# Attention with mixed heads, then two MLPs, on one core: the scores of the third and fourth chunk made at other steps, q and other loads issued at other places

## The chip, the cores and the metric

One core of a Trainium2 chip runs the whole program. The metric is the device time of one execution in microseconds (us); lower is better. Five engines work side by side, each in its own program order: TensorE (PE, with its weight loads PEld), VectorE (DVE), ScalarE (ACT), GpSimd (POOL), and SyncE (SP), which here only issues DMAs.

## The reference

Batch 2, 12 heads, 448 tokens, head size 64. Cut to what the change touches:

```python
scores = scale * np.matmul(q, k.transpose(0, 1, 3, 2))
scores = np.einsum('bhij,hg->bgij', scores, w_pre)
scores = scores - np.max(scores, axis=-1, keepdims=True)
attn = np.exp(scores)
attn = attn / (np.sum(attn, axis=-1, keepdims=True) + 1e-09)
attn = np.einsum('bhij,hg->bgij', attn, w_post)
return np.matmul(attn, v)
```

The result, as 2 x 448 tokens of 768 channels, goes through a token-and-channel-mixing MLP and then a gated MLP with a spatial gate. Neither is touched by the change.

## The kernel before, in words

**Chunks.** The query tokens of each batch are cut into four chunks (120, 120, 120 and 88 tokens), eight chunks in all, numbered x = 0 to 7. `qk(x, i)` makes the scores of head pair i (0 to 5) of chunk x: eight PE matmul instructions into a PSUM tile of two banks, and a copy of 128x896 numbers to the chunk's tile `S`, by ACT or, where the call names it, by DVE. There are two PSUM pools, psM and psB, of two such tiles each; `post` and `av` take theirs from psM, `pre` from psB.

**Steps.** A chunk is worked off in steps of 20 tokens: 6, 6, 6 and 5 per batch, 46 steps in all; chunk 2 begins at step 12, chunk 3 at step 18, chunk 4 at step 23. Each step has these parts: `b_dma` (two DMAs on SP gather the step's rows out of `S` into two of the eight ring tiles `P`, 210 KB each), `b_pre` (eight matmuls mix the heads with w_pre), `b_max` (DVE), `b_exp` (two ACT exponentials with their sums), `b_norm` (POOL: reciprocal of the sums, and w_post scaled by it), `b_post` (56 small matmuls that mix the heads with w_post and transpose), and `b_turn` (DVE copies the result into `AT`).

**Order.** The program is written out by hand in one loop over i from -5 to 45, and every engine runs its part in that order. Round i holds, in this order: `pre` of step i+2; the first `qk` that is due; `max` of i+2; `norm` of i+1; the other `qk` that are due; `post` of step i; `exp` of i+2; `turn` of i; an `av` (attention times v, 80 PE instructions) if one is due; the gather `b_dma` of step i+5; the loads listed for round i; and one move of the weight conversion (`pump`). So a gather is issued some four steps ahead of the `pre` that reads it, and `exp` of a step must be done before `pre` of two steps later may overwrite its PSUM tile.

**Scores and loads before.** Chunks 0 and 1 are scored ahead of the loop. Chunk 2's six `qk` come at rounds 1 to 6, chunk 3's at 7 to 12, chunk 4's at 13 to 17 with two at 13, and those of chunks 5 to 7 one per round at 18 to 35. Loads of q (192 KB), k (224 KB), v (512 KB) and the first weight piece (512 KB) stand in the table `loads` by round. The next batch's k tile i takes the place of this batch's, so it waits for `qk(3, i)`.

Tile names in the traces: `qk<-kn,qn` are the score matmuls, `S<-qk` their copies, `pre<-P,wp`, `nm<-pre` (max), `E<-pre,nm` (exp), `rc`, `rr`, `wt` (norm), `post<-wt,E`, `AT<-post` (turn), `av<-AT,vn`.

Of the kernel before, what the change touches and what calls it, by code (L numbers as in the profile page):

```python
# [20 lines left out]
LD, LP = 5, 2  # L21
# [10 lines left out]
def tile_kernel(ctx, tc, q, k, v, w_pre, w_post, w_tok1, w_tok2, w_ch1, w_ch2,  # L32
# [4 lines left out]
    NP = H // 2  # L37
# [136 lines left out]
    def pump(n):  # L174

        for _ in range(n):
            if wstate["conv"] < wstate["room"]:
                next(wstate["steps"], None)
# [110 lines left out]
    psM = actx.enter_context(tc.tile_pool(name="psM", bufs=2, space=PSUM))  # L289
# [11 lines left out]
    NQ = NP // QG  # L301
# [5 lines left out]
    def load_q(b, c, g, eng=nc.sync):  # L307
        t = qn[b, c, g] = qp.tile([P, QG, P], F32, tag=f"qn{g}", name=f"qn{b}_{c}_{g}", bufs=2)
        eng.dma_start(out=t, in_=q[b, :, c, g * QG:(g + 1) * QG])
# [28 lines left out]
    first = {}  # L338
# [6 lines left out]
    NB = len(steps)  # L345
# [173 lines left out]
    def add(step, fn, *a):  # L519
        extra.setdefault(step, []).append((fn, a))  # L520

    chunks = [(b, c) for b in range(B) for c in range(len(CH))]
# [25 lines left out]
    turn_over(8)  # L548

    COPIES = (nc.vector.tensor_copy,), (nc.scalar.copy,)  # L550
    scores = {}
    for x in range(NCH):
        if x < 2:
            at = [-LD - 1 + x] * NP
            for i in range(NP):
                n = x * NP + i
                add(at[i], qk, x, i, (psM, psB)[n % 2], COPIES[n % 2])
        else:
            f0, f1 = first[chunks[x - 1]] - LD, first[chunks[x]] - LD
            room = list(range(f0, f1))  # L560
            at = [room[i * len(room) // NP] for i in range(NP)]
            for i in range(NP):
                scores.setdefault(at[i], []).append((x, i))
        if x == 0:
            add(at[-1], scale_pre)
    for fn, a in extra.pop(-LD - 1):
        fn(*a)
    loads = {}
    for at, fn, *a in [(-4, load_q, 0, 2, 0), (-3, load_q, 0, 2, 1), (2, load_v, 0, 0), (4, load_q, 0, 3, 0),
                       (6, load_q, 0, 3, 1), (8, load_k, 1, 0), (9, load_q, 1, 0, 0), (9, load_k, 1, 1),  # L570
                       (10, load_k, 1, 2), (11, load_k, 1, 3), (12, load_v, 0, 1), (12, load_k, 1, 4), (13, load_k, 1, 5),
                       (10, load_q, 1, 0, 1), (14, load_v, 0, 2), (10, w_dma),
                       (15, load_const_late), (15, load_q, 1, 1, 0), (16, load_q, 1, 1, 1),
                       (18, load_q, 1, 2, 0), (20, load_q, 1, 2, 1), (24, load_v, 1, 0), (23, load_q, 1, 3, 0),
                       (26, load_v, 1, 1), (25, load_q, 1, 3, 1), (28, load_v, 1, 2)]:
        loads.setdefault(at, []).append((fn, a))
# [5 lines left out]
    TURNS_AT = {(-4, 1), (-3, 1), (-2, 1), (0, 1), (1, 1), (3, 1), (4, 1)}  # L582

    END = NB - LD
    PUMPS = {i: 1 + (i in ()) for i in range(14, NB)}
    LAST = ((0, 1, 2), (3, 4, 5))
    LAST_AT = (0, 1)
    MID_AT = (0, 3, 5)
# [1 line left out]
    for x in range(0, NCH - 2, 2):  # L590
        f0, f1 = first[chunks[x + 2]], first[chunks[x + 3]]
# [13 lines left out]
    for i in range(-LD, NB):  # L605
# [29 lines left out]
        if wstate["conv"] <= p_t2[-1]:  # L635
            pump(PUMPS.get(i, 0))
        if i + LD == first[chunks[-1]] - 1:
# [389 lines left out]
def build(shapes, manual=True):  # L1027
    import concourse.bacc as _bacc
    import concourse.tile as _tile
    import numpy as _np  # L1030
    from concourse import mybir as _mybir

    nc = _bacc.Bacc("TRN2", target_bir_lowering=False, num_devices=1, dynamic_dma_scratch_size=1024)
    args = []
    for name, (shape, dtype) in shapes.items():
        args.append(nc.dram_tensor(f"in_{name}_dram", shape, _mybir.dt.from_np(dtype), kind="ExternalInput").ap())
    for i, (shape, dtype) in enumerate(_OUTS):
        dt = _mybir.dt.from_np(_np.dtype(dtype))
        args.append(nc.dram_tensor(f"out_{i}_dram", shape, dt, kind="ExternalOutput").ap())
    with _tile.TileContext(nc) as tc:  # L1040
        if manual:
            with tc.manual_schedule():
                tile_kernel(tc, *args)
        else:
            tile_kernel(tc, *args)
    return nc
# [12 lines left out]
```

## Time and profile before

| what | value |
|---|---|
| three runs, us | 495.44, 498.73, 502.58 (median 498.73) |
| the profiled execution | 498.87 us |
| its span, first to last instruction | 497.1 us |
| granted TensorE clock, mean | 1.000 |
| PE busy | 477.4 us, 96% |
| DVE, ACT, POOL busy | 69%, 47%, 43% |
| mean DMA rate | 129 GB/s |

Attention takes roughly the first 183 us and the two MLPs the rest. "issue" in a profile row is time in which an engine waited for nothing that the profile shows. The busy time of PE is modelled and matmuls overlap, so 96% does not say that PE could not do the same work in less time.

### The profile page before, as it was taken

How to read it: one execution, taken by the hardware profiler on the slowest of the kernel's cores; microseconds unless marked ns; L12 is line 12 of the kernel's file. 1: busy time of each engine (PE TensorE's matmuls, PEld its weight loads, DVE VectorE, ACT ScalarE, POOL GpSimd, SP SyncE). 2: the span in 40 equal slices, each digit the busy share in tenths (PEclk: the TensorE clock that was granted, in tenths of full speed). 3: DMA queues.
4: the chain of work that ended last, by engine and by line, in shares of the span. 5: the costliest groups of instructions: out<-in, count | busy, mean ns of one | idle time of the engine just before them, and what ended most of it. 6: DMA issues, size and time to landing. Idle time of an engine off the chain costs nothing.

```text
span 497.1 us, 12963 instructions
## 1 busy us (share of the span) xinstructions
PE 477.4 (96%) x5482; PEld 390.2 (78%) x5482; DVE 340.7 (69%) x454; ACT 232.1 (47%) x452; POOL 211.4 (43%) x305
## 2 busy tenths in 40 slices
PE   9998899998899979999999999999999999999997
PEld 5455555555566879999999999999999998888996
DVE  3666547755775638836576678788788865897882
ACT  3577556856765435634344443333332444455320
POOL 2354544745555311581233242454445633258500
PEclk9999999999999999999999999999999999999999
DMA  5677953765443302302244253434532414004222
GB/s 181 229 235 236 264 179 119 244 204 203 162 168 100 159 4 65 127 1 69 101 127 135 98 185 113 128 106 128 172 103 86 124 57 140 20 0 128 79 79 108
DMA packets 26302, 64.17 MB, mean 129 GB/s; under 512 B 2900, under 2 KB 19844, under 8 KB 26244
## 3 DMA queue, kind: packets, MB, share of 16 engines
q1 hardware_dynamic: 26100, 63.14, 38.9%
q8 instruction: 43, 0.70, 0.6%
q10 hardware_dynamic: 144, 0.20, 0.1%
q14 instruction: 15, 0.12, 0.1%
HBM read 41.22 MB, written 2.75 MB: 88 GB/s over the span
## 4 chain that ended last, share of the span: by engine, by line
PE 87%; DVE 4%; ACT 4%; issue 3%; DMA 1%; POOL 0%; SPq 0%; POOLq 0%; ACTq 0%; DVEq 0%
PE qk L329 7%; PE av L483 6%; PE pre L369 6%; PE c2ps L662 6%; PE c1ps L662 6%; PE c2ps L664 6%; PE c1ps L664 6%; PE c1ps L663 6%; PE c2ps L663 6%; PE post L416 5%; PE av L465 2%; PE ups L663 2%; PE ups L662 2%; PE ups L664 2%; PE vps L663 2%
## 5 line engine op out<-in xcount | busy, mean ns | idle before, releaser
L157 POOL TENSOR_TENSOR wl<-cv,wh 128x768 fp32r<-128x768 f32 x28 | 53.2, 1899 | 125.1 <-ACT wh L154 93.5
L416 PEld LDWEIGHTS post<-wt,E 60*64 60x64 f32 x2520 | 46.5, 134 | 31.6 <-issue 20.1
L382 ACT ACTIVATE E<-pre,nm 128x448 f32<-128x448 f32 x90 | 56.5, 636 | 18.0 <-DVE nm L374 16.4
L416 PE MATMUL post<-wt,E 60*64 60x60 f32 x2520 | 49.9, 219 | 9.0 <-issue 7.5
L434 DVE COPY AT<-post 128x840 f32<-128x840 f32 x43 | 44.2, 1031 | 19.7 <-PE post L416 19.7
L374 DVE TENSOR_REDUCE nm<-pre 128x2 f32<-128x896 f32 (+1 forms) x46 | 48.9, 1063 | 6.9 <-PE pre L369 6.4
L369 PE MATMUL pre<-P,wp 64*64 64x448 f32 (+1 forms) x360 | 51.0, 543 | 1.7 <-DMA P<-S 0.6
L334 ACT COPY S<-qk 128x896 f32<-128x896 f32 x42 | 38.0, 907 | 31.1 <-PE qk L329 31.1
L136 DVE SCALAR_TENSOR_TENSOR cv<-raw,cv 128x768 uint32<-128x768 uint32 (+2 forms) x44 | 51.5, 1170 | 1.2
L662 PE MATMUL c1ps<-uh,wh 128*128 128x448 f32 x144 | 52.3, 363 | 0.0
L662 PE MATMUL c2ps<-r1h,wh 128*128 128x448 f32 x144 | 52.3, 363 | 0.0
L664 PE MATMUL c1ps<-uh,wl 128*128 128x448 f32 x144 | 52.2, 362 | 0.0
L664 PE MATMUL c2ps<-r1h,wl 128*128 128x448 f32 x144 | 52.2, 362 | 0.0
L663 PE MATMUL c1ps<-ul,wh 128*128 128x448 f32 x144 | 51.8, 360 | 0.0
L663 PE MATMUL c2ps<-r1l,wh 128*128 128x448 f32 x144 | 51.8, 360 | 0.0
L114 ACT ACTIVATE cv<-raw 128x768 f32<-128x768 f32 (+2 forms) x44 | 36.1, 822 | 27.8 <-POOL wl L157 20.7
L329 PE MATMUL qk<-kn,qn 64*64 64x448 f32 x384 | 48.1, 548 | 0.0
L138 DVE SCALAR_TENSOR_TENSOR cv<-raw,cv 128x768 uint32<-128x768 uint32 (+2 forms) x44 | 41.9, 951 | 1.0
L389 POOL TENSOR_SCALAR rc<-sm 128x2 f32<-128x2 f32 (+1 forms) x46 | 10.6, 231 | 73.5 <-ACT E L382 73.2
L154 ACT CAST wh<-cv 128x768 fp32r<-128x768 f32 x28 | 23.4, 836 | 34.8 <-DVE cv L138 33.8
L685 DVE SCALAR_TENSOR_TENSOR r1l<-c1ps,r1h 128x448 fp32r<-128x448 f32 x24 | 15.0, 624 | 30.6 <-ACT r1h L683 30.6
L391 POOL TENSOR_TENSOR rr<-rc,mone 128x2 f32<-128x2 f32 (+1 forms) x46 | 32.4, 705 | 3.8
(151 smaller groups left out, 1015.1 us busy)
## 6 DMA issues: line engine op xcount, KB each, us to landing
P<-S SPq DMA_DIRECT2D x88, 210.0 KB
raw<-in_w_ch_dram SPq DMA_DIRECT2D x24, 768.0 KB
vn<-in_v_dram SPq DMA_DIRECT2D x6, 512.0 KB
raw<-in_w_v_dram SPq DMA_DIRECT2D x6, 512.0 KB
raw<-in_w_u_dram SPq DMA_DIRECT2D x4, 768.0 KB
raw<-in_w_out_dram SPq DMA_DIRECT2D x6, 512.0 KB
qn<-in_q_dram SPq DMA_DIRECT2D x15, 192.0 KB
kn<-in_k_dram SPq DMA_DIRECT2D x12, 224.0 KB
```

What stands on the lines that cost most here:

```text
L136: nc.vector.scalar_tensor_tensor(fi, lo, 29, fi, op0=ALU.logical_shift_right, op1=ALU.bitwise_or)
L138: nc.vector.scalar_tensor_tensor(fi, hi, 0xC0000000, fi, op0=ALU.bitwise_and, op1=ALU.bitwise_or)
L157: nc.gpsimd.tensor_tensor(dst[1], f, f32(dst[0]), op=ALU.subtract)
L329: nc.tensor.matmul(ps[cols, j, :S], lhsT=qn[b, c, i // QG][rows, i % QG, cols], rhs=KX[b, i][rows], start=True, stop=True)
L369: nc.tensor.matmul(ps[cols, e, :S], lhsT=wp[rs], rhs=ring[(2 * i + r) % NP_BUFS][rs], start=True, stop=True)
L374: nc.vector.tensor_reduce(out=st[i]["nm"][:, :ne], in_=st[i]["pre"][:, :ne, :S], axis=AX.X, op=ALU.max, negate=True)
L382: nc.scalar.activation(t, st[i]["pre"][:, e, :S], AF.Exp, bias=st[i]["nm"][:, e:e + 1], scale=1.0, accum_out=sm[:, e:e + 1])
L416: nc.tensor.matmul(ps[HALVES[x], r, o:o + HW], lhsT=st[i]["e"][e][rs, t * 64:(t + 1) * 64], rhs=st[i]["w"][e][rs, :HW], start=True, stop=True)
L434: copy(dst, src)
L662: nc.tensor.matmul(ps, lhsT=lh, rhs=rh, start=(start and i == 0), stop=False)
L663: nc.tensor.matmul(ps, lhsT=lh, rhs=rl, start=False, stop=False)
L664: nc.tensor.matmul(ps, lhsT=ll, rhs=rh, start=False, stop=(stop and i == n - 1))
```

## The change

Three tables of the loop are written anew.

1. `QK_AT` says at which round each `qk` of chunks 2 to 7 is made. Chunk 2: rounds -2, -2, -1, -1, 0 and 1; those at rounds up to 0 are copied by ACT and DVE in turn, where all were copied by ACT. Chunk 3: rounds 3, 5, 7, 9, 11, 12. Chunk 4: as before. Chunk 5: two at 18, then 19 to 22. Chunks 6 and 7: each one round earlier, 23 to 28 and 29 to 34.
2. Chunk 2's q is loaded right behind the scores of chunk 0, ahead of the first gather; chunk 3's q at rounds 1 and 5 instead of 4 and 6; the first v tile at 9 instead of 2; the k tiles of the second batch at 10 to 15 instead of 8 to 13; its first q at 11 and 13 instead of 9 and 10; the first weight piece at 13 instead of 10.
3. The weight conversion begins at round 16 instead of 14 and makes two moves at rounds 20 and 30, so that the number of moves is the same.

```diff
     COPIES = (nc.vector.tensor_copy,), (nc.scalar.copy,)
+    QK_AT = [[-2, -2, -1, -1, 0, 1], [3, 5, 7, 9, 11, 12], [13, 13, 14, 15, 16, 17], [18, 18, 19, 20, 21, 22], [23, 24, 25, 26, 27, 28], [29, 30, 31, 32, 33, 34]]
     scores = {}
...
         else:
-            f0, f1 = first[chunks[x - 1]] - LD, first[chunks[x]] - LD
-            room = list(range(f0, f1))
-            at = [room[i * len(room) // NP] for i in range(NP)]
+            at = QK_AT[x - 2]
             for i in range(NP):
-                scores.setdefault(at[i], []).append((x, i))
+                scores.setdefault(at[i], []).append((x, i, psM, COPIES[1 - i % 2]) if at[i] <= 0 else (x, i))
...
+    for g in range(NQ):
+        load_q(0, 2, g)
     loads = {}
-    for at, fn, *a in [(-4, load_q, 0, 2, 0), (-3, load_q, 0, 2, 1), (2, load_v, 0, 0), (4, load_q, 0, 3, 0),
-                       (6, load_q, 0, 3, 1), (8, load_k, 1, 0), (9, load_q, 1, 0, 0), (9, load_k, 1, 1),
...
+    for at, fn, *a in [(1, load_q, 0, 3, 0), (5, load_q, 0, 3, 1),(9, load_v, 0, 0), (10, load_k, 1, 0), (11, load_q, 1, 0, 0), (11, load_k, 1, 1),
+                       (12, load_k, 1, 2), (12, load_v, 0, 1), (13, load_k, 1, 3), (13, load_q, 1, 0, 1),
...
-    PUMPS = {i: 1 + (i in ()) for i in range(14, NB)}
+    PUMPS = {i: 1 + (i in (20, 30)) for i in range(16, NB)}
```

PE ahead of the first `post`, before the change (`pre0` is `pre` of step 0; `qk0_2_3` is batch 0, chunk 2, head pair 3):

```order
 L329 MATMUL qk0_1_5_213<-kn0_5_117,qn0_1_1_121 64x448 x4
 L369 MATMUL pre0_229<-P0_93,wp_69 64x448 x2
 L369 MATMUL pre0_229<-P1_94,wp_69 64x448 x2
 L369 MATMUL pre1_243<-P2_95,wp_69 64x448 x2
 L369 MATMUL pre1_243<-P3_96,wp_69 64x448 x2
 L369 MATMUL pre2_265<-P4_97,wp_69 64x448 x2
 L369 MATMUL pre2_265<-P5_98,wp_69 64x448 x2
 L416 MATMUL post0_280<-wt0_0_254,E0_0_237 64x60 x12
```

The same place after it:

```order
 L329 MATMUL qk0_1_5_217<-kn0_5_117,qn0_1_1_121 64x448 x4
 L369 MATMUL pre0_229<-P0_93,wp_69 64x448 x2
 L369 MATMUL pre0_229<-P1_94,wp_69 64x448 x2
 L329 MATMUL qk0_2_0_235<-kn0_0_103,qn0_2_0_182 64x448 x4
 L329 MATMUL qk0_2_1_243<-kn0_1_107,qn0_2_0_182 64x448 x4
 L369 MATMUL pre1_256<-P2_95,wp_69 64x448 x2
 L369 MATMUL pre1_256<-P3_96,wp_69 64x448 x2
 L329 MATMUL qk0_2_2_261<-kn0_2_109,qn0_2_0_182 64x448 x4
 L329 MATMUL qk0_2_3_277<-kn0_3_113,qn0_2_1_184 64x448 x4
 L369 MATMUL pre2_290<-P4_97,wp_69 64x448 x2
 L369 MATMUL pre2_290<-P5_98,wp_69 64x448 x2
 L329 MATMUL qk0_2_4_295<-kn0_4_115,qn0_2_1_184 64x448 x4
```

Five of chunk 2's score pairs now stand between the first three `pre` and the first `post`.

SP at the first gathers, as one piece of the difference (`P0` to `P7` are the ring tiles):

```order
 L69 DMA wd_post_68<-in_w_post_dram 128x60
+L309 DMA qn0_2_0_182<-in_q_dram 128x384
+L309 DMA qn0_2_1_184<-in_q_dram 128x384
 L361 DMA P0_93<-S0_0_144 120x1x448
 L361 DMA P1_94<-S0_0_144 120x1x448
 L361 DMA P2_95<-S0_0_144 120x1x448
 L361 DMA P3_96<-S0_0_144 120x1x448
-L309 DMA qn0_2_0_223<-in_q_dram 128x384
 L361 DMA P4_97<-S0_0_144 120x1x448
 L361 DMA P5_98<-S0_0_144 120x1x448
-L309 DMA qn0_2_1_227<-in_q_dram 128x384
 L361 DMA P6_99<-S0_0_144 120x1x448
```

The two q loads moved from behind the second and third gather to ahead of the first.

SP from the gather of step 18 (round 13) to that of step 20, before:

```order
 L361 DMA P4_97<-S0_3_677 120x1x448
 L361 DMA P5_98<-S0_3_677 120x1x448
 L316 DMA kn1_5_1128<-in_k_dram 128x448
 L361 DMA P6_99<-S0_3_677 120x1x448
 L361 DMA P7_100<-S0_3_677 120x1x448
 L305 DMA vn0_2_1212<-in_v_dram 128x1024
 L361 DMA P0_93<-S0_3_677 120x1x448
```

and after:

```order
 L361 DMA P4_97<-S0_3_465 120x1x448
 L361 DMA P5_98<-S0_3_465 120x1x448
 L316 DMA kn1_3_1120<-in_k_dram 128x448
 L309 DMA qn1_0_1_1122<-in_q_dram 128x384
 L100 DMA raw0_1124<-in_w_tok1_dram 128x1024
 L361 DMA P6_99<-S0_3_465 120x1x448
 L361 DMA P7_100<-S0_3_465 120x1x448
 L316 DMA kn1_4_1208<-in_k_dram 128x448
 L305 DMA vn0_2_1210<-in_v_dram 128x1024
 L361 DMA P0_93<-S0_3_465 120x1x448
```

Between the same gathers two loads have become five.

## Rows read from the trace of the kernel before

**Rows 1.** The page's first part: engine, busy us, share of the span, instructions.

```profile
PE 477.4 (96%) x5482; PEld 390.2 (78%) x5482; DVE 340.7 (69%) x454; ACT 232.1 (47%) x452; POOL 211.4 (43%) x305
```

**Rows 2.** Busy time by stretch: length, five engines, clock, DMA share, GB/s.

```profile
20.00:57.00 37.00, 32.80 (x909) 20.77 (x912) 25.45 (x25) 26.20 (x64) 20.39 (x54) 1.00 0.75 242
57.00:96.00 39.00, 37.78 (x892) 22.13 (x886) 24.40 (x33) 25.73 (x60) 19.28 (x48) 1.00 0.58 186
...
193.00:497.00 304.00, 300.46 (x1502) 275.98 (x1500) 223.13 (x305) 117.71 (x186) 123.94 (x87) 1.00 0.32 101
```

**Rows 3.** Timeline of PE, 20 to 60 us: start, length, matmuls, idle before.

```profile
20.37 0.39 PE L416 MATMUL post<-wt,E 60*64 60x60 f32 x6
...
32.20 0.91 PE L416 MATMUL post<-wt,E 60*64 60x60 f32 x44
34.07 0.39 PE L416 MATMUL post<-wt,E 60*64 60x60 f32 x11 [0.96 <-issue]
...
38.09 0.62 PE L416 MATMUL post<-wt,E 60*64 60x60 f32 x26
39.87 0.63 PE L416 MATMUL post<-wt,E 60*64 60x60 f32 x28 [1.16 <-issue]
...
44.17 0.34 PE L416 MATMUL post<-wt,E 60*64 60x60 f32 x8
45.39 0.92 PE L416 MATMUL post<-wt,E 60*64 60x60 f32 x48 [0.88 <-issue]
...
56.38 1.08 PE L416 MATMUL post<-wt,E 60*64 60x60 f32 x56
57.64 0.44 PE L465 MATMUL av<-AT,vn 64*64 64x120 f32 x8 [0.18 <-ACT S L334]
```

**Rows 4.** The chain of waits in a late step: start, length, work.

```profile
80.04 0.75 PE pre L369 x8
80.80 0.75 PE qk L329 x8
81.55 0.81 PE post L416 x56
```

**Rows 5.** Waits, 20 to 57 us: who waited for whom, us in total, times, longest.

```profile
PE post L416 <- issue: 3.8, 4, 1.2
...
PE pre L369 <- DMA P<-S: 0.3, 1, 0.3
```

**Rows 6.** The page's third part: an instruction queue's packets and MB.

```profile
q8 instruction: 43, 0.70, 0.6%
```

**Rows 7.** Timeline of PE, 79 to 97 us: `post` of steps 17 and 23.

```profile
81.36 1.00 PE L416 MATMUL post<-wt,E 60*64 60x60 f32 x56
...
95.57 1.05 PE L416 MATMUL post<-wt,E 60*64 60x60 f32 x56
```

**Rows 8.** Groups of instructions, 20 to 57 us: busy us, mean ns | idle before.

```profile
L382 ACT ACTIVATE E<-pre,nm 128x448 f32<-128x448 f32 x26 | 16.3, 637 | 2.2 <-DVE nm L374 2.2
...
L374 DVE TENSOR_REDUCE nm<-pre 128x2 f32<-128x896 f32 x13 | 14.1, 1083 | 3.6 <-PE pre L369 3.1 <-ACT E L382 0.5
...
L434 DVE COPY AT<-post 128x840 f32<-128x840 f32 x12 | 12.4, 1034 | 8.4 <-PE post L416 8.4
L334 ACT COPY S<-qk 128x896 f32<-128x896 f32 x12 | 10.9, 906 | 9.4 <-PE qk L329 9.4
```

**Rows 9.** Groups over the whole span: the score copies of DVE.

```profile
L334 DVE COPY S<-qk 128x896 f32<-128x896 f32 x6 | 6.5, 1092 | 7.7 <-PE qk L329 7.7
```

**Rows 10.** Timeline of the DMA issues on SP: start, length of the issue.

```profile
14.94 0.45 SPq L309 DMA_DIRECT2D qn<-in_q_dram  x1
...
26.56 0.75 SPq L305 DMA_DIRECT2D vn<-in_v_dram  x1
```

**Rows 11.** The chain of waits at step 29: start, length, what.

```profile
121.84 2.11 issue
```

More of the change, by code (lines that the diff above doesn't have):

```diff
@@ L567, in tile_kernel @@
         fn(*a)
+    for g in range(NQ):
+        load_q(0, 2, g)
     loads = {}
-    for at, fn, *a in [(-4, load_q, 0, 2, 0), (-3, load_q, 0, 2, 1), (2, load_v, 0, 0), (4, load_q, 0, 3, 0),
-                       (6, load_q, 0, 3, 1), (8, load_k, 1, 0), (9, load_q, 1, 0, 0), (9, load_k, 1, 1),
-                       (10, load_k, 1, 2), (11, load_k, 1, 3), (12, load_v, 0, 1), (12, load_k, 1, 4), (13, load_k, 1, 5),
-                       (10, load_q, 1, 0, 1), (14, load_v, 0, 2), (10, w_dma),
+    for at, fn, *a in [(1, load_q, 0, 3, 0), (5, load_q, 0, 3, 1),(9, load_v, 0, 0), (10, load_k, 1, 0), (11, load_q, 1, 0, 0), (11, load_k, 1, 1),
+                       (12, load_k, 1, 2), (12, load_v, 0, 1), (13, load_k, 1, 3), (13, load_q, 1, 0, 1),
+                       (14, load_k, 1, 4), (14, load_v, 0, 2), (15, load_k, 1, 5), (13, w_dma),
                        (15, load_const_late), (15, load_q, 1, 1, 0), (16, load_q, 1, 1, 1),
```

## The prediction

> **What bounds the kernel now.** Read the page's first part first: PE is counted busy for 96% of the span [rows 1], so all the time that any edit can win without taking PE work away is in PE's idle and slowed stretches. The busy time by stretch shows where these are [rows 2]: from 193 us on, the MLPs keep PE busy for 300.5 of 304 us, and the change does not reach them; from 57 to 96 us it is 37.8 of 39; from 20 to 57 us it is 32.8 of 37, with the DMA engines at a share of 0.75 and 242 GB/s, the most of the three. That stretch is steps 0 to 12. Its first `post` starts at 20.37 us, the `post` of step 12 at 56.38 and the first `av` at 57.64 [rows 3]: 36.0 us for twelve steps, 3.0 us a step.
>
> What should a step take? In a late step that waits for nothing, `pre` takes 0.75 us, one score pair 0.75 and `post` 0.81 [rows 4], 2.32 us in all. Twelve of these are 27.8 us, so 8.2 us of the 36.0 are lost. The waits of that stretch name the loser [rows 5]: the gathers cost PE 0.3 us, so data come early enough, while `post` alone waited 3.8 us in four waits of up to 1.2 us for "issue", that is, for nothing that the profile shows. The timeline of PE gives a pattern [rows 3]: the waits fall after 44 of 56 matmuls of the `post` of step 4, after 26 of step 6's, after 8 of step 8's. They come 18 matmuls earlier every two steps. Two steps are 144 matmuls and as many weight loads; less 18 of each that is 252 PE instructions, and a few waits on semaphores. The page counts 43 packets and 0.70 MB on an instruction queue, 16 KB each [rows 6]; PE's 10,964 instructions over 43 are 255 a packet. So PE stops where its own code comes in blocks, and it does so while the DMA engines are loaded. Where they are not overloaded it need not: from step 17 to step 23, one score pair per step and the gathers running, six steps took 14.21 us [rows 7], 2.37 us each, with no stop in between.
>
> The Trainium skill's "Runtime: NRT & Kernel Launch", section "Instruction fetch mechanics", has the same block of 16 KiB and 256 instructions, fetched by a DMA queue of the sequencer's own, but calls the cost of a crossing mostly hidden. The stops of about 1 us disagree for this stretch; by that rule they would have another cause and stay, which is the first rival below.
>
> **The change part by part.**
>
> *Chunk 2's scores ahead.* Four score pairs leave rounds 2 to 6 for rounds -2 and -1, two stay in rounds 0 and 1. PE has room there: its first `post` waits for the chain of gather, max, exponential and norm. But their copies stand in that chain: on ACT one of 0.91 us ahead of each of the first three exponentials [rows 8], on DVE one of 1.09 us [rows 9] behind each of the first two max. The first `post` waits for a PSUM tile that these copies free. Followed through the queues, the copy of the first pair puts the first exponential off by 0.4 us, the second ACT copy adds up to 0.9 to what follows. I take +0.9 us for the first `post`, one ACT copy; the bounds are 0 (all hidden) and +2.0 (one ACT and one DVE copy in row).
>
> *q of chunk 2 ahead of the gathers.* It stood between gathers, two issues of about half a us, the first at 14.94 us [rows 10]. Now SP issues it while it waits for the first chunk's copies. That takes about 1 us out of SP's queue at the start; I count nothing for it, since exponential and norm end last there. It is at most a gain of 1.0.
>
> *Steps 0 to 12.* Four score pairs fewer are 4 x 0.75 = 3.0 us of PE. Chunk 3's pairs now come at 3, 5, 7, 9, 11 and 12, so that a step holds 1.57 or 2.32 us of PE work. What is late next is DVE: a max of 1.08 and a turn of 1.03 us per step [rows 8] are 2.12, and ACT has 2 x 0.64 for the exponentials, and 0.91 more in every second step. So a step cannot stay under 2.12. The transfers become fewer at the same time: of what was issued in rounds -4 to 8 (v, four q, one k, 1.5 MB), chunk 3's q alone, 0.4 MB, is left in the loop; the v issue at 26.56 us [rows 10], just ahead of the first clear stop, is gone. So the pace should be that of steps 17 to 23: 12 x 2.37 = 28.4 us, and 1.26 from the last `post` to `av` as before, 29.7 against 37.3 us: a gain of 7.6. Bounds: if all stops stay, only the 3.0 us of score pairs; if DVE alone sets the pace, 12 x 2.12 + 1.26 = 26.7, a gain of 10.6.
>
> *Loads later.* Rounds 9 to 15 now issue 4.1 MB of loads besides the gathers, where it was 3.3. The 0.75 MB more are, at the 242 GB/s of [rows 2], 3.1 us of transfer. Each load still has two rounds or more to land, one of them mostly with an `av`, so I expect no wait for k or v itself; what suffers is PE's code. Around the blocks of steps 9 to 17 the stops of before, 0.8 to 1.2 us, should grow. Half of the 3.1 us lies beside the `av` of steps 12, 14 and 16, where PE needs code more slowly (the 80 instructions of an `av` are longer ones); I take a loss of 1.5 us. The lower bound is 0; the upper is the stop of 2.11 us at step 29 [rows 11], just after a v tile and a weight piece had been issued back to back, at each of the some six blocks of these steps, 12.7 us, against four stops like those of [rows 3] now, some 3.8: 9 more.
>
> *Chunks 5 to 7 and the pump.* The same instructions one round earlier, step 18 with one pair more and step 35 with one less; as many moves of the conversion. They are covered by PE-bound steps. 0, give or take 1.0: the weight piece of round 28 moves behind a gather, which may shorten the 2.11 us stop, or the double move at round 30 may delay a norm.
>
> The sum: 0.9 - 7.6 + 1.5 = -5.2 us on the profiled execution's 498.87 (497.1 of span and 1.8 around it): **493.7 us**. That execution lies 0.1 us over the median of the three runs, so the same number stands against it.
>
> **The rivals.** *The stops stay.* If they don't come from loaded DMA engines, or if the gathers alone load them enough, only the four pairs leave the stretch: -3.0 + 0.9 = -2.1, and 496.8 us. For it speaks that the stop at 44.5 us comes when v was long in; against it the six steps without a stop [rows 7]. The Trainium skill's rule on code fetch, above, would make this the case.
>
> *All goes.* DVE's pace of 2.12 us, no delay at the start, and the late stops shorter: -10.6 + 0.5 = -10.1, 488.8 us. Against it: in no six steps of before were they that short, and DVE and PE would have to mesh without a gap.
>
> *Slower.* The loads of rounds 9 to 15 are the mechanism, PE's code blocks of steps 9 to 17 the place, the price up to 9 us as above. It decides from the point where these stops take 6.7 us more than now, which is all that the steps before have won: 498.87 + 0.9 - 7.6 + 9 = 501.2 us. For it: five loads, where there were two, between the gathers of steps 18 and 20. Against it: `av` thins out the code there, and from 57 to 96 us the DMA share was only 0.58 [rows 2], which leaves room.
>
> *The change doesn't do what it says:* the q tiles come too late for rounds -2 and -1, the scores hold up `pre`, and nothing is won: 499 us. The q buffers are free once half of chunk 0's scores are made, so I give this little.
>
> **How the numbers follow.** Forecast, a gain of 3 to 8.5 us: 0.62. The stops stay: 0.17. All goes: 0.12. Slower: 0.06. Not as said: 0.03. The range leaves out most of the slower case and the far end of "all goes": 488.5 to 499.5 us. About 2% (10 us) is what a measurement of this kernel can tell from no change; the three runs of before spread over 7 us. Of the cases only "all goes" reaches 10 us, and about all of it is needed: faster by over 2%, 0.11. Slower by over 2% would be over 508.7 us, beyond the worst case worked out: 0.02. Within 2%: 0.87.
>
> **What would show it.** Right: the first `post` at about 21.3 us and the first `av` at about 51; no or shorter waits for "issue" in steps 2 to 8; longer ones in steps 9 to 17; the distance from the first `av` to the end one or two us longer than before. Wrong: stops every 256 instructions in steps 2 to 8 as before, a first `post` after 22.5 us, or PE waiting for k or v at step 13 or later.

## The result

The changed kernel takes 490.58 us (median of five runs, 486.75 to 491.07) against 497.04 for the kernel before on the same chip (five runs, 495.17 to 502.58): a ratio of 0.985, with a 95% interval of 0.982 to 0.989, that is, 1.1 to 1.8% less. The forecast was 493.7 with a range of 488.5 to 499.5. The profiled execution took 490.66 us with a span of 488.9, against 498.87 and 497.1.

The page's first part of the changed kernel, to be read beside [rows 1]:

```profile
PE 474.2 (97%) x5482; PEld 388.2 (79%) x5482; DVE 342.8 (70%) x456; ACT 230.0 (47%) x450; POOL 210.9 (43%) x305
```

The same work in a shorter span. Busy time by stretch of the changed kernel (length, the five engines, clock, DMA share, GB/s), cut at the same places of the program as [rows 2]: steps 0 to 12, the steps behind them, the MLPs.

```profile
20.00:50.00 30.00, 28.53 (x900) 17.26 (x896) 26.23 (x27) 23.73 (x62) 20.41 (x54) 1.00 0.69 235
50.00:88.00 38.00, 35.97 (x802) 21.28 (x806) 21.94 (x27) 23.37 (x53) 18.17 (x44) 1.00 0.71 216
186.00:489.00 303.00, 298.79 (x1490) 274.50 (x1488) 221.91 (x302) 116.16 (x183) 122.47 (x87) 1.00 0.30 100
```

The first stretch is 7 us shorter. DVE is busy for 26.2 of its 30 us; before it was 25.5 of 37. The second has taken over the load: the DMA share rose from 0.58 to 0.71, and PE is idle for 2.0 of 38 us, where it was 1.2 of 39. The MLPs are unchanged.

PE in steps 0 to 12 of the changed kernel, from its timeline (start, length, matmuls, idle before), to be read beside [rows 3]:

```profile
21.15 1.04 PE L416 MATMUL post<-wt,E 60*64 60x60 f32 x56
...
27.66 0.98 PE L329 MATMUL qk<-kn,qn 64*64 64x448 f32 x8 [0.71 <-DVE AT L434]
...
30.00 1.02 PE L416 MATMUL post<-wt,E 60*64 60x60 f32 x56
...
42.70 0.33 PE L416 MATMUL post<-wt,E 60*64 60x60 f32 x3 [0.38 <-issue]
...
48.64 1.08 PE L416 MATMUL post<-wt,E 60*64 60x60 f32 x56
49.91 0.44 PE L465 MATMUL av<-AT,vn 64*64 64x120 f32 x8 [0.19 <-ACT S L334]
```

The first `post` starts at 21.15, that of step 12 at 48.64: 27.5 us, where it was 36.0. The `post` of step 4 (30.00) runs through; of PE's waits for "issue" in these steps a single one of 0.38 is left. What the steps wait for now is in the waits, to be read beside [rows 5] (who waited for whom, us in total, times, longest). The first line is of the kernel before, 20 to 57 us, the others are of the changed kernel, 20 to 50 us:

```profile
PEld post L416 <- issue: 9.0, 16, 1.3
...
PEld post L416 <- POOL wt L395: 7.1, 12, 0.9
...
PE qk L329 <- DVE AT L434: 0.7, 1, 0.7
...
PE post L416 <- issue: 0.4, 1, 0.4
```

The weight loads of all twelve `post` now wait for the norm on POOL, the last link of max, exponential and norm, where before they waited for "issue". The stops of PE have gone, and as far as the waits show, the chain beside PE sets the pace.

The same reading for every kernel of this study: the start of the first `post`, the time from there to `post` of step 12, and so on, taken from each one's timeline of PE. The experiments are named in the rows and told below.

| kernel | first `post` | 0 to 12 | 12 to 18 | 18 to 24 | 24 to 35 | 35 to 45 | `post` of 45 |
|---|---|---|---|---|---|---|---|
| before | 20.37 | 36.0 | 27.3 | 18.4 | 37.3 | 36.7 | 176.13 |
| after | 21.15 | 27.5 | 29.6 | 17.7 | 34.5 | 37.0 | 167.44 |
| after, again | 22.15 | 26.8 | 31.1 | 17.7 | 33.2 | 36.3 | 167.23 |
| q ahead alone | 19.23 | 34.1 | 26.7 | 18.4 | 37.6 | 36.7 | 172.73 |
| scores alone | 21.57 | 29.2 | 29.5 | 18.7 | 32.7 | 37.0 | 168.62 |
| loads alone | 20.49 | 32.3 | 27.5 | 17.7 | 34.0 | 37.0 | 168.93 |
| v at round 2 | 23.11 | 26.6 | 29.3 | 18.9 | 33.2 | 36.4 | 167.55 |
| code shifted | 23.90 | 32.6 | 28.0 | 18.6 | 34.1 | 36.7 | 173.82 |
| chunks 5 to 7 as before | 21.89 | 28.1 | 29.4 | 17.7 | 34.9 | 36.7 | 168.55 |
| the same, v at round 2 | 21.36 | 28.9 | 26.0 | 17.7 | 34.0 | 37.4 | 165.27 |
| the same, weights at 17 | 21.57 | 30.2 | 27.6 | 19.5 | 35.9 | 37.6 | 172.34 |
| the same, v at 6 | 21.75 | 30.0 | 26.0 | 19.6 | 36.5 | 37.6 | 171.33 |

Before against after: +0.8, -8.5, +2.3, -0.7, -2.8, +0.3, together -8.7 us up to `post` of step 45; the span is 8.2 us shorter. "After, again" is a second profile of the same kernel on another chip: it differs from the first by up to 1.5 us in a cell, so a single cell that moves by less tells nothing. "Chunks 5 to 7 as before" is the profile from its second chip; the one from the first is of a slow run (493.89 us, where its other three took 486.27 to 487.64) and is left out.

### The profile page after: what moved, and what is told of

Read it like the earlier page. It is cut to its first block, busy times and chain, and to the rows that moved or that the text cites. A ratio compares the mean times of both kernels' runs of the same rounds, so it can differ in the third digit from the quotient of the medians.

```text
span 488.9 us, 12962 instructions
## 1 busy us (share of the span) xinstructions
PE 474.2 (97%) x5482; PEld 388.2 (79%) x5482; DVE 342.8 (70%) x456; ACT 230.0 (47%) x450; POOL 210.9 (43%) x305
## 4 chain that ended last, share of the span: by engine, by line
PE 88%; DVE 4%; ACT 4%; issue 2%; POOL 1%; POOLq 0%; ACTq 0%; DVEq 0%
PE qk L329 7%; PE av L483 6%; PE c2ps L662 6%; PE c1ps L662 6%; PE c2ps L664 6%; PE c1ps L664 6%; PE c1ps L663 6%; PE c2ps L663 6%; PE pre L369 6%; PE post L416 5%; PE ups L663 2%; PE av L465 2%; PE ups L662 2%; PE vps L662 2%; PE ups L664 2%
## 5 line engine op out<-in xcount | busy, mean ns | idle before, releaser
L416 PE MATMUL post<-wt,E 60*64 60x60 f32 x2520 | 48.7, 219 | 4.5 <-issue 2.4
L369 PE MATMUL pre<-P,wp 64*64 64x448 f32 (+1 forms) x360 | 47.6, 542 | 0.5 <-issue 0.4
L334 ACT COPY S<-qk 128x896 f32<-128x896 f32 x40 | 36.1, 908 | 22.6 <-PE qk L329 22.4
L329 PE MATMUL qk<-kn,qn 64*64 64x448 f32 x384 | 45.6, 548 | 0.9 <-DVE AT L434 0.7
```

What stands on the lines that cost most here:

```text
L329: nc.tensor.matmul(ps[cols, j, :S], lhsT=qn[b, c, i // QG][rows, i % QG, cols], rhs=KX[b, i][rows], start=True, stop=True)
L369: nc.tensor.matmul(ps[cols, e, :S], lhsT=wp[rs], rhs=ring[(2 * i + r) % NP_BUFS][rs], start=True, stop=True)
L416: nc.tensor.matmul(ps[HALVES[x], r, o:o + HW], lhsT=st[i]["e"][e][rs, t * 64:(t + 1) * 64], rhs=st[i]["w"][e][rs, :HW], start=True, stop=True)
```

## The experiments

The kernel before is timed anew on each chip (497.67 us, 495.85 and 495.38), and each kernel is compared with it there.

**q ahead alone.** The kernel before, and of the change only this:

```diff
+    for g in range(NQ):
+        load_q(0, 2, g)
     loads = {}
-    for at, fn, *a in [(-4, load_q, 0, 2, 0), (-3, load_q, 0, 2, 1), (2, load_v, 0, 0), (4, load_q, 0, 3, 0),
+    for at, fn, *a in [(2, load_v, 0, 0), (4, load_q, 0, 3, 0),
```

> The kernel before with one edit: chunk 2's two q loads go ahead of the first gather; every other load, score pair and pump as before. The prediction counted nothing for this, at most 1 us: then 496.5 to 497.7. Rival: the queue of transfers that the later loads meet is shorter by these two (0.4 MB, 1.6 us at 242 GB/s) from 15 us on, and PE's code blocks of steps 2 to 8 come in time: 2 to 4 us faster, about 494.5, with the stops of steps 4 and 6 under 0.5 us.

Measured: 493.0 us, ratio 0.9946 (0.9908 to 0.9985), a gain of 0.7 to 4.6 us. Its timeline of PE still has the stops, at the very matmuls of [rows 3]:

```profile
29.42 0.91 PE L416 MATMUL post<-wt,E 60*64 60x60 f32 x44
31.57 0.39 PE L416 MATMUL post<-wt,E 60*64 60x60 f32 x11 [1.24 <-issue]
...
35.59 0.62 PE L416 MATMUL post<-wt,E 60*64 60x60 f32 x26
37.39 0.63 PE L416 MATMUL post<-wt,E 60*64 60x60 f32 x28 [1.17 <-issue]
...
41.68 0.33 PE L416 MATMUL post<-wt,E 60*64 60x60 f32 x8
42.62 0.92 PE L416 MATMUL post<-wt,E 60*64 60x60 f32 x48 [0.61 <-issue]
```

After 44, 26 and 8 matmuls, as before. Two loads of 192 KB that no longer stand between the first gathers are worth some 2.7 us, without touching the stops of steps 4 and 6. So the rival's size came true and its reason did not. In the profile the gain starts with the first two steps: 2.4 and 2.3 us from `post` to `post`, where the kernel before took 3.1 and 3.0; loads alone, which has the same q loads, has the same 2.4 and 2.3.

**Scores alone.** The changed kernel's `QK_AT` with the q loads that it needs; v, k, the other loads and the conversion as before. Against the changed kernel:

```diff
-    for at, fn, *a in [(1, load_q, 0, 3, 0), (5, load_q, 0, 3, 1),(9, load_v, 0, 0), (10, load_k, 1, 0), (11, load_q, 1, 0, 0), (11, load_k, 1, 1),
+    for at, fn, *a in [(2, load_v, 0, 0), (1, load_q, 0, 3, 0),
+                       (5, load_q, 0, 3, 1), (8, load_k, 1, 0), (9, load_q, 1, 0, 0), (9, load_k, 1, 1),
...
-    PUMPS = {i: 1 + (i in (20, 30)) for i in range(16, NB)}
+    PUMPS = {i: 1 + (i in ()) for i in range(14, NB)}
```

> The changed score rounds with the q loads that they need; v, k, the second batch's q, the weight piece and the conversion stand where they stood before. Theory A (the loads moved out of rounds 2 to 8 are what frees PE's code blocks, and that is the larger part): only 2 to 3 us faster than the kernel before, about 494.5, and stops of about 1 us for issue are back in steps 2 to 8. Theory B (taking score pairs out of the steps is the larger part, by PE and ACT work): 6 us or more faster, about 491, the first av within 1 us of the changed kernel's 49.9.

Measured: 491.42 us, ratio 0.9881 (0.9829 to 0.9932). Its timeline of PE:

```profile
21.57 1.05 PE L416 MATMUL post<-wt,E 60*64 60x60 f32 x56
...
45.21 0.86 PE L416 MATMUL post<-wt,E 60*64 60x60 f32 x43
48.41 0.39 PE L416 MATMUL post<-wt,E 60*64 60x60 f32 x11 [2.35 <-issue]
```

From step 0 to step 11 are 23.64 us, 2.15 a step, with no stop, although v (512 KB) is loaded at round 2. So fewer scores in the loop are enough for the pace, and that v is harmless then. Theory B has the time right. The bill comes in step 11, one stop of 2.35 us, and with it the first `av` starts at 52.21, not within 1 us of 49.9 as theory B had it.

**Loads alone.** The changed kernel's loads and conversion, q ahead included, with every score where it was before:

```diff
-    QK_AT = [[-2, -2, -1, -1, 0, 1], [3, 5, 7, 9, 11, 12], [13, 13, 14, 15, 16, 17], [18, 18, 19, 20, 21, 22], [23, 24, 25, 26, 27, 28], [29, 30, 31, 32, 33, 34]]
+    QK_AT = [[1, 2, 3, 4, 5, 6], [7, 8, 9, 10, 11, 12], [13, 13, 14, 15, 16, 17], [18, 19, 20, 21, 22, 23], [24, 25, 26, 27, 28, 29], [30, 31, 32, 33, 34, 35]]
```

> The changed loads and conversion, with every score pair at its round of before. Theory A: 4 to 6 us faster than the kernel before, about 492, with the stops of steps 2 to 8 shorter than 0.5 us. Theory B: 0 to 1.5 us faster, about 496.5, and steps 0 to 12 still take 35 us or more.

Measured: 491.92 us, ratio 0.9887 (0.9815 to 0.9959). Its timeline of PE:

```profile
35.46 0.62 PE L416 MATMUL post<-wt,E 60*64 60x60 f32 x26
37.26 0.63 PE L416 MATMUL post<-wt,E 60*64 60x60 f32 x28 [1.17 <-issue]
...
41.56 0.34 PE L416 MATMUL post<-wt,E 60*64 60x60 f32 x8
42.50 0.92 PE L416 MATMUL post<-wt,E 60*64 60x60 f32 x48 [0.61 <-issue]
```

The stop of step 4 has gone with the v load; those of steps 6 and 8 stand. The time is that of theory A, but not its reason: two stops are still over 0.5 us. Of the whole, each half of the change gives about six of its six and a half to seven microseconds. Set against q ahead alone, which both contain, the scores add some 0.6% and the later loads 0.6%; with the 0.5% of q that makes 1.8%, and the whole gave 1.5 and, on the second chip, 1.2%. The intervals, half a per cent and more each way, do not settle whether anything is lost in between.

**v at round 2.** The changed kernel with the first v where it was before:

```diff
-    for at, fn, *a in [(1, load_q, 0, 3, 0), (5, load_q, 0, 3, 1),(9, load_v, 0, 0), (10, load_k, 1, 0), (11, load_q, 1, 0, 0), (11, load_k, 1, 1),
+    for at, fn, *a in [(1, load_q, 0, 3, 0), (5, load_q, 0, 3, 1),(2, load_v, 0, 0), (10, load_k, 1, 0), (11, load_q, 1, 0, 0), (11, load_k, 1, 1),
```

> The changed kernel with the first v tile loaded at round 2 as before, and all else as changed. Theory A: one or two stops of 0.5 to 1 us are back in steps 3 to 6; what rounds 9 to 12 win back is less, so 0.5 to 1.5 us slower than the changed kernel. Theory B: within 0.5 us of it, no stop in steps 3 to 6.

Measured: 489.23 us, ratio 0.9842 (0.9789 to 0.9895), no slower than the changed kernel as far as the intervals tell. Steps 0 to 12 took 26.6 us, no more than with v at round 9. The theory that v at round 2 was what stopped PE in those steps falls for the changed order: with the new scores no stop comes back in steps 3 to 6. With the old scores v counts for the stop of step 4 alone, since loads alone keeps those of steps 6 and 8 without it.

**Code shifted.** The kernel before with 32 more PE instructions ahead of everything (16 matmuls of 64 columns and their weight loads; the idle matmuls do no work for the result):

```diff
-            nc.tensor.matmul(idle[:, 0, :P], lhsT=ident, rhs=ident, start=True, stop=True)
+            nc.tensor.matmul(idle[:, 0, :64], lhsT=ident, rhs=ident[:, :64], start=True, stop=True)
-    turn_over(8)
+    turn_over(16)
```

> The kernel before, with sixteen idle matmuls of 64 columns ahead of the first scores instead of eight of 128, so that all later PE code lies 32 instructions further back. If PE stops at the ends of 256-instruction blocks of its code, the stops fall 16 matmuls earlier: after 28 of 56 in the post of step 4 and after 10 in that of step 6, no longer after 44, 26 and 8. If they hang on what the post works with (a scaled weight, an exponential, a PSUM tile), they stay after 44, 26 and 8. Time within 2 us of the kernel before either way.

Measured (one run): 497.07 us. The kernel before in step 11 and in step 29, from its timeline of PE:

```profile
53.00 0.91 PE L416 MATMUL post<-wt,E 60*64 60x60 f32 x44
54.69 0.39 PE L416 MATMUL post<-wt,E 60*64 60x60 f32 x11 [0.78 <-issue]
...
120.86 0.98 PE L416 MATMUL post<-wt,E 60*64 60x60 f32 x52
123.95 0.33 PE L416 MATMUL post<-wt,E 60*64 60x60 f32 x4 [2.11 <-issue]
```

and the kernel with shifted code in step 11, and in the step that answers to the other:

```profile
53.13 0.66 PE L416 MATMUL post<-wt,E 60*64 60x60 f32 x28
54.62 0.62 PE L416 MATMUL post<-wt,E 60*64 60x60 f32 x27 [0.83 <-issue]
...
121.89 1.00 PE L416 MATMUL post<-wt,E 60*64 60x60 f32 x56
```

The stop of step 11 came after 28 matmuls, 16 earlier than after 44: with 16 matmuls and 16 weight loads more ahead of it, that is the same place of PE's code. Step 15 agrees: its stop comes after 48 matmuls in q ahead alone and after 32 here. So the stops belong to places in the code, 256 instructions apart, and not to an operand. The stops foretold for steps 4 and 6 did not show at their new places or at their old ones.

The packets of 16 KB on the instruction queue [rows 6] say what PE waits for there, since the trace has the start and the length of each. In the twelve profiles of the table PE has 52 waits for "issue" of 0.2 us or more between 20 and 137 us. Each of the 52 ended 1.3 to 1.7 us after such a packet had ended, and by and large, the later the packet began, the longer was the stop: 0.2 us where it began 2.6 us ahead of the stop, 0.96 where it began 1.55 ahead, 2.65 where it began 0.07 ahead. So PE waits for its code.

The Trainium skill's "Runtime: NRT & Kernel Launch", section "Instruction fetch mechanics", calls the crossing mostly hidden. Here that holds for a part of the crossings only: of some twenty in that stretch the kernel before stopped at nine, for 0.23 to 2.11 us, the changed kernel at four and, in its second profile, at two. The second thing to see is that the late stops of [rows 11] are gone in this profile, with the loads and the scores as before: steps 24 to 35 took 34.1 us instead of 37.3. The same edit also put the first `post` off by 3.5 us, and `post` of step 12 came at 56.53 all the same, where it was 56.38: the later steps had fewer stops. Why they had fewer is not shown.

**Chunks 5 to 7 as before.** The changed kernel with one pair per round at 18 to 35, run on two chips, and on the first of them the changed kernel itself again beside it:

```diff
-    QK_AT = [[-2, -2, -1, -1, 0, 1], [3, 5, 7, 9, 11, 12], [13, 13, 14, 15, 16, 17], [18, 18, 19, 20, 21, 22], [23, 24, 25, 26, 27, 28], [29, 30, 31, 32, 33, 34]]
+    QK_AT = [[-2, -2, -1, -1, 0, 1], [3, 5, 7, 9, 11, 12], [13, 13, 14, 15, 16, 17], [18, 19, 20, 21, 22, 23], [24, 25, 26, 27, 28, 29], [30, 31, 32, 33, 34, 35]]
```

> The changed kernel with the score pairs of chunks 5 to 7 at their rounds of before, 18 to 35, one per round. If the two pairs at round 18 are what made step 18 take 4.2 us where it took 2.3, step 18 is back at 2.3 to 2.8 and the kernel 0.5 to 1.5 us faster than the changed one. Rival: the pairs only move, step 35 and those behind it give back what step 18 gains, and the time stays within 0.5 us.

> The changed kernel itself, on the chip and in the rounds of the three above, as the thing they are compared with: 487 to 491 us, first post at 21.2 us, first av at 49 to 52.

> The changed kernel with chunks 5 to 7 scored as before, a second time, on the same chip as the two above. If the two pairs at round 18 cost what the earlier run showed, 487 to 488.5 us and a step 18 of 2.3 us. If that run's gain was chance, 489.5 to 491.

Measured: 487.57 us, ratio 0.9821 (0.9776 to 0.9866), on the first chip; 490.49, ratio 0.9882 (0.9841 to 0.9924), for the changed kernel beside it; 491.44, ratio 0.9899 (0.9864 to 0.9935), on the second. The step of two pairs, in the timeline of PE of the changed kernel:

```profile
76.03 1.84 PE L329 MATMUL qk<-kn,qn 64*64 64x448 f32 x16
78.21 1.04 PE L416 MATMUL post<-wt,E 60*64 60x60 f32 x56 [0.34 <-POOL rr L391]
```

Both pairs stand ahead of `post` of step 18; from the `post` ahead of it to this one are 4.2 us, 3.6 in the second profile, and 2.3 with one pair. But the last step of the row of pairs is cheaper by as many matmuls, and the time shows no gain that held on the second chip: the first gain of 3 us was chance, or smaller than the runs can tell. On the second chip the changed kernel itself was not run beside it.

**The same, v at round 2.** Chunks 5 to 7 as before, and the first v at round 2, by the same edit as above.

> The changed kernel with chunks 5 to 7 as before and the first v tile at round 2 again, a candidate for a better version. If fewer loads in rounds 9 to 12 help and v at round 2 costs nothing once the scores are out of the way: 1 to 2.5 us faster than the changed kernel. If v at round 2 brings the stops back: no faster than it.

Measured: 488.64 us, ratio 0.985 (0.9813 to 0.9887), 1.9 us under the changed kernel beside it by the medians, with intervals that overlap. Its profile has the smallest sum of the table, with the stops moved: its timeline of PE has stops of 0.56, 0.48 and 1.11 us in steps 6 to 10 and nothing up to step 24.

**Weights at round 17.** Chunks 5 to 7 as before, the first weight piece at round 17 instead of 13, the conversion from round 19 with five double moves; and then the first v at round 6 as well:

```diff
-                       (14, load_k, 1, 4), (14, load_v, 0, 2), (15, load_k, 1, 5), (13, w_dma),
+                       (14, load_k, 1, 4), (14, load_v, 0, 2), (15, load_k, 1, 5), (17, w_dma),
...
-    PUMPS = {i: 1 + (i in (20, 30)) for i in range(16, NB)}
+    PUMPS = {i: 1 + (i in (20, 26, 30, 32, 38)) for i in range(19, NB)}
```

> The changed kernel with chunks 5 to 7 scored as before, and the first weight piece (512 KB) issued at round 17 instead of 13, the conversion from round 19. If the loads of rounds 9 to 15 are what stops PE in steps 12 to 17, taking an eighth of their 4.1 MB out should bring steps 12 to 18 to about 26 us (before: 27.3) and the time 1 to 2 us under that of the same kernel without this edit, 487.6 us there, so 486 to 487. If the stops come by chance wherever a code block ends while anything is loaded, the time stays at 487 to 488.5 and a stop of 1 us or more shows elsewhere.

> As the one ahead of it, and the first v tile (512 KB) at round 6 instead of 9, so that one megabyte of the loads has left rounds 9 to 15. If the amount there decides, another 0.5 to 1 us faster, 485.5 to 486.5, with no stop over 1 us after step 10. If a load costs the same stop wherever it is issued, no faster than the one ahead of it: 487 to 488.5, with a stop of about 0.5 to 1 us in steps 6 to 8.

Measured: 493.3 us, ratio 0.9959 (0.9923 to 0.9994), and 492.87, ratio 0.9942 (0.9912 to 0.9972); 1.4 to 1.9 us slower by the medians than the same kernel without these edits on that chip, with intervals that overlap. Both expectations were wrong, though the steps they speak of became shorter: 12 to 18 took 27.6 and 26.0 us, instead of 29.4. The weights need not be the reason, since the kernel with them at 13 and v at round 2 also has 26.0. The profiles lost time on both sides of these steps: 0 to 12 took 30.2 and 30.0 us instead of 28.1, with one stop of 2.65 and one of 1.83, and 18 to 45 took 93.0 and 93.7 instead of 89.2. The waits of PE from 80 to 176 us say where the latter went, first without the two edits, then with weights at 17:

```profile
PE post L416 <- POOL wt L395: 1.7, 3, 0.7
...
PE post L416 <- POOL wt L395: 2.6, 4, 0.7
PE post L416 <- DVE AT L434: 1.6, 1, 1.6
```

and so does its chain of waits (start, length, what), where a conversion of 1.94 us on POOL holds up what follows, and a second piece on DVE stands ahead of a max:

```profile
85.94 1.94 POOL cv L132
...
90.27 0.60 DVE cv L136
90.86 1.01 DVE nm L374
```

With the conversion begun three rounds later, its moves were packed two to a round into steps whose max and norm had no room for them. That this, and not the weight piece, cost the time is read from these waits; no run has one without the other.

## Why the prediction was right, and where it was not

*What bounds steps 0 to 12.* Right. The code blocks were the cause of the stops: the shifted code moved a stop by the 16 matmuls that were put ahead of it, every stop ended 1.3 to 1.7 us behind a packet of code, and the changed kernel's steps run through where [rows 3] stop. But the stops are only a part of what was won: PE's waits for "issue" in `post` fell from 3.8 us to 0.4, and the four score pairs are 3.0 us by the prediction's count.

*Steps 0 to 12, the term of 7.6.* Right in kind, 0.9 too small: 36.0 us became 27.5, a gain of 8.5, and 9.2 in the second profile. The pace of 2.37 us that it rests on was read too low: one of the six steps, step 22, holds eight tokens only, and the five full ones from `post` 17 to `post` 22 took 12.2 us, 2.44 each. The term should have been 6.7. Of its two reasons, fewer score pairs and fewer transfers, the runs bear out the first: scores alone, with v still at round 2, has no stop up to step 10, while loads alone keeps the stops of steps 6 and 8. The floor named for DVE, 2.12 us a step, was nearly reached; scores alone ran at 2.15, the changed kernel at 2.29. Against "all goes" it had been said that PE and DVE would have to mesh without a gap; they did so more nearly than was granted.

*Chunk 2's scores ahead, the term of 0.9.* Right in this profile, 0.8. But in the table the first `post` lies anywhere from 19.2 to 23.9, and it is 1.0 later for the same kernel in its second profile, so the agreement is within what varies by itself.

*q ahead of the gathers, counted at nothing.* Mis-sized: alone it gave 2.7 us (0.7 to 4.6). In its profile the first `post` wins 1.1 us (19.23 against 20.37), which the text gave as a bound and then did not count; but loads alone, with the same q loads, has 20.49, so this may be chance. The rest was won in steps 0 to 12 (34.1 against 36.0 us), from the first two on, where two loads less stand among the first gathers. That was not considered at all.

*Loads later, the term of 1.5.* Steps 12 to 18 took 2.3 us longer, and 3.8 in the second profile, but not all of this is the term. The step up to `post` of step 18, which now holds two score pairs, has 1.9 and 1.3 us of it. Up to `post` of step 17 the loss is 0.4 us (25.3 against 25.0) and, in the second profile, 2.5. The 1.5 of the sum lies between two profiles of one kernel, so that its size is neither shown nor refuted. Nor did the runs show the later loads as the cause: counted up to `post` of step 17, scores alone, with the loads where they were, loses 0.9 us, and loads alone, with the scores where they were, 0.2. Both are less than what two profiles of one kernel differ by. The two stops of the second profile show what such stops can cost there, in its timeline of PE:

```profile
58.47 0.64 PE L416 MATMUL post<-wt,E 60*64 60x60 f32 x32
61.45 0.57 PE L416 MATMUL post<-wt,E 60*64 60x60 f32 x24 [2.33 <-issue]
...
66.50 0.87 PE L416 MATMUL post<-wt,E 60*64 60x60 f32 x47
68.83 0.38 PE L416 MATMUL post<-wt,E 60*64 60x60 f32 x9 [1.45 <-issue]
```

In the first profile the same places, after 32 matmuls of step 14 and 47 of step 15, cost nothing and 0.43 us. The sixfold stop of 2.11 us, which the rival "slower" rested on, did not come; 3.8 us in a profile is the most that these steps of the changed kernel showed.

*Chunks 5 to 7 and the pump, 0 give or take 1.* This is the step that failed. Steps 18 to 35 gained 3.5 us, and 4.8 in the second profile, nearly all of it in steps 24 to 35. Some 0.7 us of it is only moved, since the last of these steps no longer holds the pair that now stands ahead of `post` of step 18. The rest is stops that have gone, such as that of [rows 11]. The prediction had named what might shorten it, the weight piece of round 28 moving behind a gather, and held the gain to 1.0.

Two things can take these stops away, and the runs have each without the other. One is a shift of PE's code, by which its blocks end at other places of the steps: the shifted code has 34.1 us in steps 24 to 35 and scores alone 32.7, both with the loads and the conversion of before in these steps. The other is the loads and the conversion: loads alone has the PE instructions of the kernel before in the same order, stops in steps 6 and 8 at the same matmuls, and has 34.0; chunks 5 to 7 as before, which has that order from round 18 on, has 34.9. The kernel q ahead alone has neither and keeps a stop of 2.37 us. The DMA issues on SP at round 28 of the kernel before, and behind them those of loads alone (start, length of the issue):

```profile
117.28 0.34 SPq L305 DMA_DIRECT2D vn<-in_v_dram  x1
117.71 0.37 SPq L100 DMA_DIRECT2D raw<-in_w_tok_dram  x1
...
113.17 0.34 SPq L305 DMA_DIRECT2D vn<-in_v_dram  x1
113.89 1.68 SPq L361 DMA_DIRECT2D P<-S  x2
115.66 0.43 SPq L100 DMA_DIRECT2D raw<-in_w_tok_dram  x1
```

The weight piece has moved behind a gather, 2.5 us after v where it was 0.4, and in the changed kernel the two stand as far apart (111.12 and 113.62). The `post` of step 29, which stopped for 2.11 us after 52 matmuls, runs through in loads alone:

```profile
116.75 1.02 PE L416 MATMUL post<-wt,E 60*64 60x60 f32 x56
```

The changed kernel has both the shift and the moved piece, so the runs do not say which of them won its two to three microseconds; that the weight piece, and not another load, is what counts in loads alone is an inference too. The mechanism that the prediction named is therefore not refuted; what failed is its limit of 1.0 us, and that a shift of the code was not thought of. The chain of waits of the changed kernel has one stop left, to be read beside [rows 11]:

```profile
120.26 1.63 issue
```

In its second profile there is none.

*The rivals.* The stops of steps 2 to 8 did not stay. "All goes" was a gain of 10.1 us and the forecast one of 5.2. On the same chip 6.5 were measured by the medians, and the ratio's interval is 5.3 to 9.2, so the time lies between the two. Two parts of "all goes", a pace near DVE's and shorter late stops, are in what happened. The time within 2% and the range held.

*The signs.* The first `post` came at 21.15, the first `av` at 49.91, and the waits for "issue" in steps 2 to 8 went, as foretold. Longer ones in steps 9 to 17 came in the second profile only (2.33 and 1.45 us; 0.43 at most in the first), and from the first `av` to the end are 439.0 us, where it was 439.5, not one or two more. That the time came out near the forecast, with the terms of 0.9 and 1.5 inside what varies by itself and some 3 us won in late steps that the sum had at nothing, is in part luck.

*What stays open* is why a packet of code comes late. Three kernels of this study run the same PE instructions up to step 11 with the same loads around: the changed kernel, in two profiles with no stop of note at that block's end, chunks 5 to 7 as before with 1.82 us, weights at 17 with 2.65. In the changed kernel the packet began at 44.63 and 44.85 us and PE came to the block's end at 47.0 and 47.4; in the other two it began at 45.75 and 46.02, and PE was there at 46.4 and 46.1. What held the packet back for that microsecond no run shows.

## What to carry to other kernels

Where PE waits for "issue" at places some 256 of its instructions apart while DMA queues are full, move transfers or PE work out of that stretch, and then look at every later stretch too, since both the block ends and the time of arrival have moved. Taking work out of a stretch can hand the loads around it to the next one (here the DMA share there rose from 0.58 to 0.71): count what is still on the way when PE gets there sooner. Before a gain elsewhere is put down to the edit at hand, look for a run that has the gain without it. A background job that is started later has to be packed tighter, and that can be paid on the engines that it shares with the chain.

## What the runs showed of the hardware

A stop can be followed by some microseconds at half the granted clock, and need not be. Scores alone, around its stop of 2.35 us from 46.06 on (busy time by stretch, the column behind the engines is the granted clock):

```profile
40.00:50.00 10.00, 7.53 (x220) 4.31 (x212) 6.81 (x8) 6.78 (x18) 6.94 (x19) 0.97 0.90 253
50.00:60.00 10.00, 9.75 (x184) 6.37 (x180) 3.49 (x4) 4.31 (x9) 1.64 (x5) 0.86 0.82 235
```

A clock of 0.97 and 0.86 of 2.4 GHz over ten microseconds each is 0.6 and 2.8 us at 1.2 GHz: 3.4 in all, in steps 11 and 12. By that count it cost up to 1.7 us besides the stop. Weights at 17 had the same behind its stop of 2.65 us. The changed kernel in its second profile did not show it behind its stop of 2.33 us, nor did chunks 5 to 7 as before behind one of 2.47 us up to 57.79. The same view of that last kernel:

```profile
56.00:60.00 4.00, 2.21 (x22) 1.03 (x22) 1.09 (x1) 0.42 (x1) 0.00 (x0) 1.00 0.89 216
```

The clock stays at 1.00. So the length of a stop alone does not say whether the clock falls.
